# Seven half-block products for eight in a second feed-forward: one level of Strassen's scheme in a fused attention and feed-forward kernel

## The chip, the core and the metric

The kernel runs on one core of one Trainium2 chip. The metric is device time in microseconds (us) from start to end of one launch, as the median of three runs. A profile is one execution of its own, recorded by the hardware profiler; its times are read as us from the start of its span (first to last instruction). Engines are named as in the profile: PE is TensorE (matmuls), PEld its weight loads, DVE is VectorE, ACT is ScalarE, POOL is GpSimd, and SP issues the DMA transfers.

## What is computed

Three layers follow each other over 2304 tokens (4 sequences of 576).

```python
scores = q @ k.T / 8                       # 4 x 8 heads, 576 x 576, head size 64
scores = where(scores >= max - tau, scores, -1e9)
x = softmax(scores) @ v                    # heads joined: 2304 x 512
h = x @ w_in                               # 512 -> 1024
solu = h * softmax(h)
y = (layernorm(solu) * g_ln) @ w_out       # 1024 -> 512: y is 2304 x 512
h2 = y @ w2_in                             # 512 -> 2048
g = h2 * tanh(softplus(h2))                # "mish"
out = g @ w2_out                           # 2048 -> 512
```

The four weight matrices come as 64-bit floats. The kernel turns them into 32-bit floats on the chip.

## The kernel before

**An order made by a planner.** The code adds tasks (`plan.add`): an engine, a duration by a formula (`act`, `dve`, `gps`, `pe`, `dma`), the tasks it depends on, and the buffer slots that it takes or uses. `Plan.run` then tries `TURNS` rounds of list scheduling, forward and backward, with several weights (`WAITS`, `AVOID`), keeps the shortest order and writes the instructions in that order into the queue of each engine. So each engine's queue is a fixed order, and an instruction that waits holds all behind it. `ORDER` breaks ties between engines. Tasks marked `port=True` on VectorE and all GpSimd tasks are never planned at the same time.

**Words.** Each factor of the feed-forward matmuls is split into a high word (a copy that rounds to the type float32r, by ScalarE) and a low word (the difference, by VectorE or GpSimd). A product is then three matmuls: high by high, low by high, high by low.

**Attention** (`s_tile`, `turn`, `pv`) goes over 16 pairs of heads. **The first feed-forward** goes over 18 tiles of 128 tokens: `moe_h` (two output banks of 512 columns, 12 matmuls each), `layer_norm`, `moe_t` (transposes through PSUM into `LH`, `LL`) and, for each pair of tiles, `moe_y` (8 pieces of 12 matmuls, 256 wide), whose result `y` leaves as `yh` and `yl` to `y_hi`, `y_lo` in DRAM. Its pieces stand between those of attention where the order allows it.

**The second feed-forward** goes over four quarters `q` of the 2048 features, and within each over units of tokens `work`: for the first quarter six units of 256 tokens (`U0`), which may run while the first feed-forward isn't finished, then units of up to 512. `ff_in(c)` multiplies 48 matmuls into banks `h2` (`L981`), applies mish (`L986`), splits into `gh` (`L987`) and `gl` (`L988`); `ff_out(c)` multiplies 48 into `o2` (`L1007`), and VectorE adds the result into `acc` (`L1031`), which holds all output in SBUF, or ScalarE copies it there for the first quarter. The six early units put theirs by way of `part` in DRAM.

**The weights** of all four matrices are fetched in blocks of 128 by 256 by `convert` (`L474` to `L497`: two ScalarE or VectorE operations, three of VectorE, one addition by GpSimd). Those of the second feed-forward are converted in `split_w2(q)`, right into the tiles `AH`, `AL`, `BH`, `BL` of their quarter (`L924`, `L926`), of which two sets stand in turn.

**Buffers open in three steps**, as one stage's memory is given to the next: `open_a` when attention's scores are done (weight tiles of even quarters), `open_b` when its outputs are stored (buffers of the early units and six banks of PSUM), `open_c` when the first feed-forward has stored `y` (the rest).

## Time and profile before

| | |
|---|---|
| median of three runs | 913.32 us (912.12 to 914.53) |
| the profiled execution | 908.55 us |
| its span | 906.8 us |
| TensorE busy | 889.1 us |
| VectorE busy | 528.1 us |
| ScalarE busy | 522.0 us |
| GpSimd busy | 335.7 us |
| bytes moved by DMA | 122.28 MB, mean 135 GB/s |

Busy time counts an engine's instructions once where they overlap, so the sum of single durations is larger. A matmul's shown duration runs past the start of the next: what one costs is read from the distance of starts, or from a group in the chain of work that ended last (so many in so many us). The share of the DMA engines is a mean over sixteen.

### The profile page before, as it was taken

Reading aid. Unit: us, or ns where it says so; the run is one execution under the profiler, and the core shown is the slowest. Engines: PE = TensorE matmul, PEld = TensorE weight load, DVE = VectorE, ACT = ScalarE, POOL = GpSimd, SP = SyncE. Lnnn points to the kernel's source line nnn. Section 1 sums busy time; section 2 is a strip of 40 time slices with the busy share of each in tenths; the row PEclk is TensorE's granted clock in tenths of the full one; section 3 lists DMA queues with packets and bytes.
Section 4 is the critical chain, followed back from the end, with each engine's and each line's share of the span. In section 5 each row is a group of like instructions: output and inputs, shape, how many; then the busy total and the mean of one; then the engine's idle time right before and its main releaser. Section 6 shows DMA issues by size and latency. Waiting matters only on the chain.

```text
span 906.8 us, 15748 instructions
## 1 busy us (share of the span) xinstructions
PE 889.1 (98%) x5611; PEld 735.7 (81%) x5611; DVE 528.1 (58%) x1204; ACT 522.0 (58%) x1096; POOL 335.7 (37%) x470
## 2 busy tenths in 40 slices
PE   8889999999999999999999999999999999999998
PEld 4555566779878888979999999988888888888887
DVE  7998787888886787567743421445544354222222
ACT  5888788989887777567854533554432333221220
POOL 2565657787555553255411102343331234000000
PEclk9999999999999999999999999999999999999999
DMA  5434534355334431247333138954444444223211
GB/s 190 157 132 150 163 133 133 96 162 159 104 120 128 133 103 54 71 118 249 103 117 105 59 105 270 362 182 151 157 158 139 151 151 140 93 71 120 89 47 70
DMA packets 102173, 122.28 MB, mean 135 GB/s; under 512 B 11968, under 2 KB 75728, under 8 KB 102096
## 3 DMA queue, kind: packets, MB, share of 16 engines
q1 hardware_dynamic: 101952, 121.28, 41.7%
q8 instruction: 44, 0.72, 0.3%
q14 instruction: 33, 0.27, 0.1%
q10 hardware_dynamic: 144, 0.00, 0.0%
HBM read 99.16 MB, written 22.09 MB: 134 GB/s over the span
## 4 chain that ended last, share of the span: by engine, by line
PE 87%; ACT 3%; DVE 2%; POOL 1%; DMA 1%; issue 1%; SPq 0%; DVEq 0%; POOLq 0%; ACTq 0%
PE o L1007 16%; PE h L981 15%; PE p_mo L817 11%; PE p_mo L748 10%; PE p_ta L697 7%; PE h2b L981 7%; PE o2b L1007 6%; PE p_ta L649 5%; PE st L614 4%; PE st L605 3%; PE p_mo L796 2%; ACT e L621 1%; DVE e L624 1%; PE p_ta L652 1%; DVE m L620 1%
## 5 line engine op out<-in xcount | busy, mean ns | idle before, releaser
L497 POOL TENSOR_TENSOR cf<-cf,cl 128x256 uint32<-128x256 uint32 x96 | 74.4, 777 | 134.7 <-DVE cf L495 107.5
L624 DVE SCALAR_TENSOR_TENSOR e<-st,m,e 128x576 f32<-128x576 f32 x132 | 106.8, 815 | 26.7 <-ACT e L621 17.1
L620 DVE TENSOR_REDUCE m<-st 128x1 f32<-128x576 f32 x132 | 97.9, 752 | 24.8 <-PE st L614 13.7
L621 ACT ACTIVATE e<-st,m 128x576 f32<-128x576 f32 x132 | 97.2, 742 | 24.8 <-DVE m L620 23.2
L649 PE MATMUL p_ta<-ident,e 128*128 128x128 f32 x576 | 86.2, 277 | 5.4 <-ACT ey L632 2.4
L649 PEld LDWEIGHTS p_ta<-ident,e 128*128 128x128 f32 x576 | 65.7, 140 | 26.0 <-ACT ey L632 6.6
L817 PE MATMUL p_mo<-LH,W2H 128*128 128x256 f32 x288 | 83.4, 290 | 0.0
L817 PE MATMUL p_mo<-LL,W2H 128*128 128x256 f32 x288 | 81.5, 283 | 0.0
L817 PE MATMUL p_mo<-LH,W2L 128*128 128x256 f32 x288 | 81.4, 283 | 0.0
L623 POOL TENSOR_SCALAR m<-m,cs 128x1 f32<-128x1 f32 x144 | 42.4, 296 | 87.4 <-DVE m L620 75.5
L1031 DVE TENSOR_TENSOR acc<-acc,o 128x512 f32<-128x512 f32 x36 | 24.8, 688 | 70.5 <-PE o L1007 70.3
L748 PE MATMUL p_mo<-W1H,XH 128*128 128x512 f32 x144 | 60.8, 422 | 0.0
L986 ACT ACTIVATE n<-h 128x512 f32<-128x512 f32 x36 | 21.5, 597 | 63.6 <-PE h L981 62.5
L817 PEld LDWEIGHTS p_mo<-LH,W2H 128*128 128x128 f32 x288 | 55.1, 191 | 2.0 <-issue 1.9
L748 PE MATMUL p_mo<-W1H,XL 128*128 128x512 f32 x144 | 56.5, 393 | 0.0
L748 PE MATMUL p_mo<-W1L,XH 128*128 128x512 f32 x144 | 56.3, 391 | 0.0
L1007 PE MATMUL o<-gh,BH 128*128 128x256 f32 (+1 forms) x178 | 56.0, 315 | 0.0
L1007 PE MATMUL o<-gh,BL 128*128 128x256 f32 (+1 forms) x178 | 55.7, 313 | 0.0
L1007 PE MATMUL o<-gl,BH 128*128 128x256 f32 (+1 forms) x178 | 55.7, 313 | 0.0
L817 PEld LDWEIGHTS p_mo<-LH,W2L 128*128 128x128 f32 x288 | 55.2, 192 | 0.2
L817 PEld LDWEIGHTS p_mo<-LL,W2H 128*128 128x128 f32 x288 | 55.1, 191 | 0.0
L484 ACT ACTIVATE cl<-cr 128x256 uint32<-128x256 uint32 x96 | 40.9, 433 | 22.1 <-DMA cr<-w_in 16.4
(157 smaller groups left out, 2550.7 us busy)
## 6 DMA issues: line engine op xcount, KB each, us to landing
y5h<-y_hi SPq DMA_DIRECT2D x26, 512.0 KB, 4.8
y5l<-y_lo SPq DMA_DIRECT2D x26, 512.0 KB, 6.8
cr<-w_in SPq DMA_DIRECT2D x48, 256.0 KB, 3.6
cr<-w_out SPq DMA_DIRECT2D x48, 256.0 KB, 3.0
V<-v SPq DMA_DIRECT2D x16, 320.0 KB, 3.5
Q<-qq SPq DMA_DIRECT2D x16, 320.0 KB, 3.2
K<-kk SPq DMA_DIRECT2D x16, 320.0 KB, 2.9
y2h<-y_hi SPq DMA_DIRECT2D x10, 512.0 KB, 4.7
```

Source lines behind the costliest of these rows:

```text
L484: t2 = add("ACT", act(CW), lambda: SC.activation(cl.tile, cr.tile[:, :, 0], ACTF.Copy, scale=2.0 ** -29), [t_f], [cl], [cr])
L497: t = add("POOL", gps(CW), lambda: G.tensor_tensor(cf.tile, cf.tile, cl.tile, ALU.add), [t4, t2], use=[cl, cf])
L620: t = add("DVE", dve(S), lambda: V.tensor_reduce(m.tile[:, 2:3], x(), AX.XY, ALU.max, negate=True), [t], [m], [st])
L621: a = add("ACT", act(S, True) + 0.1, lambda: SC.activation(et(), x(), ACTF.Exp, bias=m.tile[:, 2:3]), [t], [e] if h == 0 else (), [st, m, ...
L623: b = add("POOL", 0.26, lambda: G.tensor_scalar(m.tile[:, 1:2], m.tile[:, 2:3], -1.0, nt8, ALU.mult, ALU.add), [t], use=[m])
L624: t = add("DVE", dve(S) + 0.06, lambda: V.scalar_tensor_tensor(et(), x(), m.tile[:, 1:2], et(), ALU.is_ge, ALU.mult, accum_out=sr.tile[:, ...
L649: TE.transpose(tp.tile[:, k * 128:(k + 1) * 128], e.tile[:, o:o + 128], ident)
L697: TE.matmul(acc.tile[h * 64:h * 64 + 64, :w], v.tile[:, k, h], r, start=(k == 0), stop=(k == KT))
L748: TE.matmul(h.tile, l.tile[:, kt], r[:, kt, j * 512:(j + 1) * 512], start=(kt == 0 and x == 0), stop=(kt == KD - 1 and x == 2))
L817: TE.matmul(y.tile[:, :PN], l[:, k, cs], r.tile[:, k], start=(k == 0 and x == 0), stop=(k == KF - 1 and x == 2))
L981: TE.matmul(h.tile[:, a * w:(a + 1) * w], l.tile[:, k, s], r.tile[:, k], start=(k == 0 and x == 0), stop=(k == KD - 1 and x == 2))
L1007: TE.matmul(o.tile[:, a * w:(a + 1) * w], l.tile[:, k, ds], r.tile[:, k % n * w:(k % n + 1) * w], start=(k == 0 and x == 0), stop=(k == FG ...
```

## The change

The second feed-forward's two products are made by one level of Strassen's scheme (in Winograd's form). A factor is cut in two by two half blocks. Seven products of sums of half blocks stand for the eight products of half blocks, and the four blocks of the result are sums of the seven; partial sums grow in the PSUM bank itself, where a bank is copied out and the next product is added to it.

- **Units.** Tokens go in 3 units of 768 (two halves of 384: each matmul is 384 wide). The 2048 features go in 8 groups of 256. `VISITS` gives the order of units and quarters: unit 0 with quarters 0 and 1, unit 1 with 1 and 0, unit 2 with all four, then units 0 and 1 again with 3 and 2, and 2 and 3.
- **Block sums of the weights** are made once, when they are converted: four VectorE operations on blocks of 128 by 128 give seven blocks from four, stored to `w2c` in DRAM as one word. They no longer wait for a tile of their quarter. A chunk that is loaded (`load_w`) is split there: the high word by ScalarE, the low one by VectorE (A) or GpSimd (B). The last group or quarter loaded is kept for the next visit.
- **Block differences of y** are made in `moe_y` by four VectorE operations for 256 tokens, split into two words (`words7`) and stored to `yc`; a visit loads seven chunks of its unit.
- **`ff_in`** makes seven products of six matmuls in three banks; ScalarE copies three partial sums, VectorE adds in three, mish is applied to four blocks, four differences give the seven blocks of the second factor (three by VectorE, one by GpSimd), and each is split in two words.
- **`ff_out`** makes 14 products of six matmuls in six banks. Every product's bank is added into `acc` (or copied, where it is the first); `acc` holds one unit, goes to `part` between the two visits of units 0 and 1, and to `out` at the end.
- **Buffers.** `open_a` now waits for the end of attention and gives the banks, the A and y chunks; `open_b` waits for the last matmuls of `moe_h` (`HT`) and gives the buffers for the banks' copies and the words of the second factor; `open_c` waits for the last `y` and gives B chunks, `acc` and two more banks.
- The planner runs 40 rounds for 80, with one more weight, and breaks ties with TensorE first. `convert` has four fetch buffers for two.

The core of the diff:

```diff
-    TURNS = 80
+    TURNS = 40
     WAITS = 20.0, 250.0
     ISSUE, LATENCY = 0.65, 0.92
-    LOAD, AVOID = 1.3, (3.0, 150.0)
+    LOAD, AVOID = 1.3, (3.0, 30.0, 150.0)
...
-    ORDER = {e: k for k, e in enumerate(("SP", "ACT", "POOL", "DVE", "PE", "-"))}
+    ORDER = {e: k for k, e in enumerate(("PE", "DVE", "ACT", "POOL", "SP", "-"))}
...
-    NG = 4
-    FG = KF2 // NG
     NP = NT // PN
     M0 = 4
-    LATE = 0
-    U0 = 6
+    TU = 3 * PN
+    TH = TU // 2
+    NU = NT // TU
+    RAW = (0,1)
+    NQ = KF2 // 2
...
+    yc = [dram.tile([7, 128, 2, TU // PN, 2, 128], F32, name=f"yc{u}") for u in range(NU)]
+    part = [dram.tile([KD, 128, TU], F32, name=f"part{u}") for u in range(NU)]
+    w2c = [[dram.tile([128, 7, 1 if x in RAW else 2, 256], F32, name=f"w2c{x}{g}") for g in range(NQ)] for x in range(2)]
...
-    b_cr = buf("cv", "cr", [128, CW, WN], U32 if WN == 2 else F32, 2)
+    b_cr = buf("cv", "cr", [128, CW, WN], U32 if WN == 2 else F32, 4)
...
+            if into:
+                at, n, slots, order = into
+                wide = lambda x: x.tile.rearrange("p (a b) -> p a b", a=n)
+                return add("POOL", gps(CW), lambda: G.tensor_tensor(at(), wide(cf), wide(cl), ALU.add), [t4, t2],
+                           slots if order is None else [], [cl, cf, *slots], order=[order])
...
+    def words7(eng, e, cost, hi, x, t, dst, n, split):
+
+        out = []
+        for c in split:
+            m = n * (c.stop - c.start)
+            a = add("ACT", act(m), lambda c=c: SC.activation(hi.tile[:, c], f(x.tile[:, c]), ACTF.Copy), [t], [] if out else [hi], [hi, x])
+            b = add(e, cost(m), lambda c=c: eng.tensor_tensor(x.tile[:, c], f(x.tile[:, c]), f(hi.tile[:, c]), ALU.subtract), [a], use=[hi, x], port=True)
+            out.append((a, b))
+        return [add("SP", dma(128 * 7 * n * 4), lambda w=w, y=y: D(dst(w), f(y.tile)), [o[w] for o in out], use=[y]) for w, y in ((0, hi), (1, x))]
+
+    WLO = V, "DVE", dve
+    ALL, HALVES = (slice(0, 7),), (slice(0, 4), slice(4, 7))
+    b_ws, b_wh = buf("ws", "ws", [128, 7, 128], F32R, 2), buf("ws", "wh", [128, 7, 128], F32R, 2)
+    for g in range(NQ):
+        for x, src in enumerate((w2_in, w2_out)):
+            WST[x, g] = []
+            for k in range(2):
+                ws, wh, ts = b_ws.new(), b_wh.new() if x not in RAW else None, []
+                for j in range(2):
+                    at = lambda ws=ws, j=j: ws.tile.bitcast(U32)[:, j:7:4 + j]
+                    row, cols = ((2 * j + k) * 128, (g * 256, g * 256 + 128)) if x == 0 else ((2 * g + j) * 128, (k * 128, 256 + k * 128))
+                    ts.append(convert(src, row, cols, None, into=(at, 2, [ws], ts[0] if ts else None)))
+                add7 = lambda o, a, b, op, ws=ws: (dve(128), lambda: V.tensor_tensor(*(f(ws.tile[:, z]) for z in (o, a, b)), op))
+                t = chain("DVE", [add7(3, 4, 6, ALU.add), add7(2, 3, 0, ALU.subtract), add7(5, 1, 2, ALU.subtract), add7(4, 0, 4, ALU.subtract)], ts, use=[ws], port=True)
+                if x in RAW:
+                    WST[x, g].append(add("SP", dma(128 * 7 * 512), lambda ws=ws, x=x, g=g, k=k: D(w2c[x][g][:, :, 0, k * 128:k * 128 + 128], f(ws.tile)), [t], use=[ws]))
+                    continue
+                WST[x, g] += words7(*WLO, wh, ws, t, lambda w, x=x, g=g, k=k: w2c[x][g][:, :, w, k * 128:k * 128 + 128], 128, ALL)
...
-        yh, yl = (b.new() for b in b_yy)
-        a = add("ACT", act(PN, True), lambda: SC.activation(yh.tile, y.tile[:, :PN], ACTF.Copy), [t], [yh], [y])
-        b = add("DVE", dve(PN), lambda: V.tensor_tensor(yl.tile, y.tile[:, :PN], f(yh.tile), ALU.subtract), [a], [yl], [yh, y])
-        YST.setdefault(p, []).append(add("SP", dma(PN * 512), lambda: D(y_hi[p][cs, :], f(yh.tile)), [a], use=[yh]))
-        YST[p].append(add("SP", dma(PN * 512), lambda: D(y_lo[p][cs, :], f(yl.tile)), [b], use=[yl]))
+        if c == 0:
+            YS[p] = b_ys.new(), []
+        ys, ts = YS[p]
+        j, k = divmod(c, 2)
+        ts.append(add("ACT", act(PN, True), lambda: SC.activation(
+            f(ys.tile)[:, j:j + 5:4, k * 128:k * 128 + 128], y.tile[:, :PN].rearrange("p (a b) -> p a b", a=2), ACTF.Copy),
+            [t], [] if c else [ys], [y, ys], order=ts[:1]))
+        if c < KD - 1:
+            return
+        sub = lambda o, a, b: (dve(256), lambda: V.tensor_tensor(*(f(ys.tile[:, z]) for z in (o, a, b)), ALU.subtract))
+        t = chain("DVE", [sub(3, 4, 0), sub(2, 5, 3), sub(4, 5, 4), sub(6, 1, 2)], ts, use=[ys], port=True)
+        u, z = divmod(p, TU // PN)
+        dst = lambda w: yc[u].rearrange("c q w z k n -> q c w z (k n)")[:, :, w, z]
+        YST[p] = words7(V, "DVE", dve, b_yh.new(), ys, t, dst, 256, HALVES)
...
+    NA, NB, NL, NR, NX, NC, NF = 9, 22, 14, 15, 3, 6, 9
+    o_a = opens(open_a, end_c3 + list(XST.values())[-2:] + [t for x in b_any.slots for t in x.users if t.eng != "PE"])
+    o_b = opens(open_b, [o_a] + HT[-4:])
+    o_c = opens(open_c, [o_b] + [t for ts in YST.values() for t in ts][-4:] + [t for ts in TEV.values() for t in ts][-16:])
+    ff = [Bank(lambda n=n: P[n], f"{n}{k}") for n, m in (("hoa", 6), ("hob", 2)) for k in range(m)]
+    for k in ff:
+        k.after = o_a if k in ff[:6] else o_c
+    b_f = Buf(None, "", [128, 512], F32, banks=ff)
+    b_a, b_b = (buf(p, n, [128, 2, 256], F32R, k) for p, n, k in (("fa", "A7", NA), ("fc", "B7", NB)))
+    b_y, b_yx = (buf(p, n, [128, 2, TU // PN, 2, 128], F32R, k) for p, n, k in (("fa", "y7", 7), ("fc", "y7x", NX)))
+    ring_y = [b_y] * 7
+    b_gl, b_gh = buf("fb", "gl", [128, TH], F32R, NL), buf("fb", "gh", [128, TH], F32R, NR)
+    b_gf = buf("fb", "gf", [128, TH], F32, NF)
+    b_ac = buf("fc", "acc", [128, TU], F32, NC)
...
+    words = (0, 0), (1, 0), (0, 1)
+    YC, GC, AC, CO, PA, AL, BL = ({} for _ in range(7))
+    VISITS = (0, (0,1)), (1, (1,0)), (2, (0,1,2,3)), (0, (3,2)), (1, (2,3))
...
+    def load_w(b, x, g, c, gate):
+        w = b.new()
+        if x in RAW:
+            t = add("SP", dma(128 * 1024), lambda: D(f(w.tile[:, 1]), w2c[x][g][:, c, 0]), WST[x, g] + [gate], [w])
+            t = add("ACT", act(256), lambda: SC.activation(w.tile[:, 0], f(w.tile[:, 1]), ACTF.Copy), [t], use=[w])
+            eng, n, cost = SPLIT[x]
+            return w, add(n, cost(256), lambda: eng.tensor_tensor(w.tile[:, 1], f(w.tile[:, 1]), f(w.tile[:, 0]), ALU.subtract), [t], use=[w], port=True)
...
+    def ff_in(z, g):
+        A = AL.pop(g, None) or [load_w(b_a, 0, g, c, o_a) for c in range(7)]
+        AL.clear()
+        AL[g] = A
+        X, Y, Z = (b_f.new() for _ in range(3))
...
+        p1 = p(0, X, True, [])
+        c1 = copy(X, s[0], p1)
+        p2 = p(1, Y, True, [])
+        g11 = mish(s[0], plus(Y, s[0], [c1, p2]))
+        p6 = p(2, X, False, [c1])
+        c2 = copy(X, s[1], p6)
+        p5 = p(3, Z, True, [])
+        p7 = p(4, X, False, [c2])
+        c3 = copy(X, s[2], p7)
+        c22 = plus(Z, s[2], [c3, p5])
+        p3 = p(5, Z, False, [c22])
+        g12 = mish(s[1], plus(Z, s[1], [c2, p3]))
+        g22 = mish(s[2], c22)
+        p4 = p(6, X, False, [c3])
+        g21 = mish(s[5], p4, X)
+        t1 = minus(0, s[3], s[1], s[0], [g11, g12], True)
+        t3 = minus(1, s[1], s[2], s[1], [t1, g22])
+        t2 = minus(2, s[4], s[2], s[3], [t1, g22], True)
+        t4 = minus(3, s[6], s[5], s[4], [t2, g21], True)
+        out = {}
+        for c, x, first, deps in ((0, 0, g11, [t1]), (5, 2, g22, [t2, t3]), (3, 3, t1, [t2]), (4, 1, t3, []),
+                                  (2, 4, t2, [t4]), (1, 5, g21, [t4]), (6, 6, t4, [])):
+            h, l, x = b_gh.new(), b_gl.new(), s[x]
+            a = add("ACT", act(TH), lambda h=h, x=x: SC.activation(h.tile, full(x), ACTF.Copy), [first], [h], [h, x])
+            e, cost, eng = ("POOL", gps, G) if c in LOWP else ("DVE", dve, V)
+            out[c] = h, l, add(e, cost(TH), lambda h=h, l=l, x=x, eng=eng: eng.tensor_tensor(l.tile, full(x), f(h.tile), ALU.subtract), [a, *deps], [l], [h, l, x], port=True)
+        GC[z, g] = out
...
+        def put(e, i, t, x, deps, first):
+            ac = AC[v, e, i]
+            to = lambda: ac.tile.rearrange("q (z t n) -> q z t n", t=2, n=128)[:, :, t]
+            fr = lambda: x.tile[:, :TH].rearrange("q (z n) -> q z n", n=128)
+            if begins and first and not more[0]:
...
+        E = range(2)
+        p1 = [p(0, e, X[e], True, []) for e in E]
+        r1 = [put(e, 0, 0, X[e], [p1[e]], True) for e in E]
+        p2 = [p(1, e, Y[e], True, []) for e in E]
+        [put(e, 0, 0, Y[e], [p2[e], r1[e]], False) for e in E]
+        p6 = [p(2, e, X[e], False, [r1[e]]) for e in E]
+        r2 = [put(e, 0, 1, X[e], [p6[e]], True) for e in E]
+        p5 = [p(3, e, Z[e], True, []) for e in E]
+        p7 = [p(4, e, X[e], False, [r2[e]]) for e in E]
+        r3 = [put(e, 1, 1, X[e], [p7[e]], True) for e in E]
+        a2 = [put(e, 1, 1, Z[e], [p5[e], r3[e]], False) for e in E]
+        p3 = [p(5, e, Z[e], False, [a2[e]]) for e in E]
+        [put(e, 0, 1, Z[e], [p3[e], r2[e]], False) for e in E]
+        p4 = [p(6, e, X[e], False, [r3[e]]) for e in E]
+        [put(e, 1, 0, X[e], [p4[e]], True) for e in E]
+        if ends:
+            for i in range(2):
+                for e in E:
+                    r0 = (e + 2 * i) * 128
+                    to = (lambda e=e, i=i: part[u][e + 2 * i]) if more[1] else (lambda r0=r0: out[r0:r0 + 128, u * TU:(u + 1) * TU])
+                    PA[u, e, i] = add("SP", dma(512 * TU), lambda e=e, i=i, to=to: D(to(), AC[v, e, i].tile),
...
+    MINUS = [{'D': ('DVE', dve(TH)), 'P': ('POOL', gps(TH))}[k] for k in 'DPDD']
+    SPLIT = ((V, "DVE", dve),(G, "POOL", gps))
+    LOWP = ()
+    for z, (_, qs) in enumerate(VISITS):
+        load_y(z)
+        for q in qs:
+            for g in (2 * q + 1, 2 * q) if q == qs[0] and z else (2 * q, 2 * q + 1):
+                ff_in(z, g)
+            ff_out(z, q)
```

## Rows read from the trace of the kernel before

**Rows 1.** The page, first part: busy us, share, instructions.

```profile
PE 889.1 (98%) x5611; PEld 735.7 (81%) x5611; DVE 528.1 (58%) x1204; ACT 522.0 (58%) x1096; POOL 335.7 (37%) x470
```

**Rows 2.** The longest wait of TensorE: us, times, longest us.

```profile
PE st L605 <- DVE e L624: 4.1, 4, 2.0
```

**Rows 3.** Busy time by stage, granted clock, DMA share, GB/s.

```profile
0.00:125.00 125.00, 112.30 (x728) 66.26 (x729) 105.85 (x252) 98.77 (x223) 65.58 (x125) 1.00 0.50 160
125.00:400.00 275.00, 273.94 (x1956) 223.44 (x1956) 210.73 (x476) 223.80 (x479) 157.65 (x212) 1.00 0.36 113
400.00:550.00 150.00, 150.00 (x1107) 142.49 (x1104) 76.29 (x181) 85.30 (x167) 41.51 (x42) 1.00 0.39 124
550.00:907.00 357.00, 352.82 (x1827) 303.46 (x1826) 135.19 (x296) 114.10 (x230) 70.91 (x94) 1.00 0.45 148
```

**Rows 4.** The chain that ended last: start, us, what.

```profile
534.50 11.52 PE p_mo L817 x96
...
655.85 2.72 PE o2b L1007 x12
```

**Rows 5.** TensorE groups by form (second feed-forward): count, busy us, mean ns.

```profile
L981 PE MATMUL h<-y5h,AH 128*128 128x512 f32 x124 | 48.3, 390 | 0.0
...
L981 PE MATMUL h<-y2h,AH 128*128 128x256 f32 x136 | 39.1, 287 | 0.0
```

**Rows 6.** The timeline of VectorE from 400 us: start, us, instruction.

```profile
402.17 0.69 DVE L802 TENSOR_TENSOR LL<-p_mo,LH 128x512 fp32r<-128x512 f32 x1 [1.09 <-ACT LH L801]
402.78 0.15 DVE L766 RECIPROCAL ln<-ln 128x1 f32<-128x1 f32 x1
...
411.44 0.42 DVE L828 TENSOR_TENSOR yl<-p_mo,yh 128x256 fp32r<-128x256 f32 x1
411.78 0.41 DVE L495 SCALAR_TENSOR_TENSOR cf<-cr,cz 128x256 uint32<-128x256 uint32 x1
```

**Rows 7.** VectorE's groups by form: busy us, mean ns, idle before.

```profile
L495 DVE SCALAR_TENSOR_TENSOR cf<-cr,cz 128x256 uint32<-128x256 uint32 x96 | 46.4, 490 | 8.4 <-POOL AL L926 5.5
...
L1031 DVE TENSOR_TENSOR acc<-acc,o 128x512 f32<-128x512 f32 x36 | 24.8, 688 | 70.5 <-PE o L1007 70.3
...
L988 DVE TENSOR_TENSOR gl<-n,gh 128x512 fp32r<-128x512 f32 x28 | 19.8, 717 | 23.6 <-ACT gh L987 23.6
```

**Rows 8.** The timeline of ScalarE, two stretches at 500 and 549 us.

```profile
502.44 1.09 ACT L801 ACTIVATE LH<-p_mo 128x512 fp32r<-128x512 f32 x2 [0.23 <-PE p_mo L796]
...
549.43 0.71 ACT L924 ACTIVATE AH<-cf 128x256 fp32r<-128x256 f32 x2
```

**Rows 9.** ScalarE's groups by form.

```profile
L801 ACT ACTIVATE LH<-p_mo 128x512 fp32r<-128x512 f32 x36 | 21.3, 599 | 9.3 <-PE p_mo L796 8.6
...
L924 ACT ACTIVATE AH<-cf 128x256 fp32r<-128x256 f32 x32 | 12.6, 410 | 8.7 <-POOL cf L497 8.7
```

**Rows 10.** GpSimd's groups by form.

```profile
L926 POOL TENSOR_TENSOR BL<-cf,BH 128x256 fp32r<-128x256 f32 x32 | 24.9, 788 | 19.6 <-ACT BH L924 19.6
...
L737 POOL TENSOR_TENSOR XL<-XR,XH 128x512 fp32r<-128x512 f32 x18 | 23.2, 1291 | 50.0 <-ACT XH L736 50.0
```

**Rows 11.** Busy time in stretches of 25 us, two of them.

```profile
50.00:75.00 25.00, 22.25 (x151) 13.03 (x149) 24.31 (x58) 21.59 (x52) 14.68 (x26) 1.00 0.45 143
...
575.00:600.00 25.00, 25.00 (x151) 22.38 (x150) 10.46 (x31) 11.65 (x25) 9.64 (x13) 1.00 0.83 280
```

**Rows 12.** The timeline of SP's queue from 549 to 556 us.

```profile
551.81 0.50 SPq L968 DMA_DIRECT2D y5l<-y_lo  x1
```

**Rows 13.** DMA issues: count, KB each, us to landing.

```profile
y_hi<-yh SPq DMA_DIRECT2D x36, 128.0 KB, 1.9
...
out<-acc SPq DMA_DIRECT2D x18, 256.0 KB, 2.1
```

**Rows 14.** The timelines of VectorE and GpSimd at 35 us.

```profile
35.68 1.48 DVE L495 SCALAR_TENSOR_TENSOR cf<-cr,cz 128x256 uint32<-128x256 uint32 x1
...
35.47 1.41 POOL L711 TENSOR_TENSOR xo<-xo,rx 128x576 f32<-128x576 f32 x1 [0.68 <-DMA rx<-rd]
```

More of the change, by code (lines that the diff above doesn't have):

```diff
@@ L507, in halves @@
         return put
[L509 to L512 removed]
+    W1T, W2T, WST = {}, {}, {}
     for c in range(0, FF, CW):
@@ new lines, with product, go @@
+    b_ac = buf("fc", "acc", [128, TU], F32, NC)
+    def product(e, terms, x, new, deps, use, stop, order=None):
+        def go():
+            steps = [(l, r) for a, b in terms for l, r in zip(a(), b())]
+            for n, (l, r) in enumerate(steps):
+                TE.matmul(x.tile[:, :TH], l, r, start=new and n == 0, stop=stop and n == len(steps) - 1, skip_group_check=True)
+        return add("PE", pe(3 * len(terms) * e, TH), go, deps, [x] if new else [], [x, *use], order=[order])
+    words = (0, 0), (1, 0), (0, 1)
```

267 lines of the change are left out of this document (89 added, 178 removed).

## The prediction

> **What bounds the kernel now.** I read the page's first part, then the waits of TensorE, then the stage windows, then the chain. TensorE is busy 889.1 of 906.8 us, no other engine over 58% [rows 1]. The reader is to see in the waits that TensorE hardly ever waits for data: the longest total is 4.1 us, in attention [rows 2]. The stage windows say where the 17.7 us of gaps lie: 12.7 in the first 125 us, 1.1 up to 400, none between 400 and 550, and 4.2 in the last window, which is the end [rows 3]. In the chain the second feed-forward is one dense run of matmul groups at two prices: twelve 512-wide ones in 2.72 us (226.7 ns each) and 96 of 256 columns in 11.52 us (120.0 ns each) [rows 4]. The price is linear: 256 more columns cost 106.7 ns, and 13.3 ns come with each matmul. The granted clock is 1.00 in every window [rows 3], the upper level (2.4 GHz), so nothing is to be had there. What shortens the kernel is work taken off TensorE, as long as the other engines keep its queue fed.
>
> **The matmuls.** By the code's list of units there are 13 of 512 tokens and 10 of 256, each with 48 matmuls in and 48 out for its quarter; [rows 5] show one form of each width (124 and 136 of them, a part). That is 1248 x 0.2267 + 960 x 0.120 = 398.1 us. After: 24 pairs of unit and 256-wide feature group make 7 products of 6 matmuls going in (1008), and 12 visits to a quarter make 14 products of 6 coming out (1008): 2016, all 384 wide. No row has that width. Per column as the 512-wide ones it would be 170.0 ns (342.7 us, a gain of 55.4); as the 256-wide ones 180.0 (362.9, a gain of 35.2). On the line between them it is 173.4 ns, 349.5 us: **a gain of 48.6 us**. I take the line, since both widths fit it exactly. It sits on the path: 906.8 - 48.6 = 858.2.
>
> **VectorE.** Each operation's length overlaps the next: a 512-wide subtraction of 0.69 us is followed after 0.61, a 256-wide one of 0.42 after 0.34 [rows 6]. So 384 costs 0.475, 128 about 0.205. Removed: 72 subtractions for gl, 54 additions into acc (both 512) and 36 for yl (256) [rows 6, 7]: 44 + 33 + 12 = 89 us. Added: 24 x 13 of 384 in ff_in (3 additions from PSUM, 3 differences, 7 low words) = 148; 144 additions into acc = 68; 140 splits of A chunks at 256 (20 loads of a group by 7) = 48; 128 block sums of weights at 128 = 26; block differences of y, 36 at 256 = 12, and their low words, 9 x (1024 + 768) = 18. Together 320. VectorE goes from 528 to 759 us, 88% of 858. It lies beside TensorE's work; that is the cover, and a thin one.
>
> **ScalarE and GpSimd.** Two LH copies of 512 take 1.09 us and two AH copies of 256 take 0.71, single ones 0.60 and 0.41: steps of 0.49 and 0.30, so 0.40 for 384 [rows 8, 9]. Removed 144 + 18 of 512 and 64 of 256 (99 us); added 24 x 14 of 384 (134), 252 splits (76), 24 copies into acc (10), y's high words (19): 522 to 662 us, 77%. GpSimd loses 64 subtractions of 256 at 0.79 (50 us), gains 112 for B (88) and 24 of 384 (between 0.79 and 1.29, about 1.04; 25) [rows 10]: 336 to 399 us, 46%. Both are hidden by TensorE; without that cover they would cost their time, but VectorE would be first to show it.
>
> **DMA and SP's queue.** The 64 fetches of second weights move ahead, past attention's loads, with 32 stores of 459 KB behind them; y's stores grow from 9.4 to 16.5 MB. The share there is 0.36 to 0.50 [rows 3], so I cost them at nothing. In the second feed-forward the loads are 18.4 (A) + 14.7 (B) + 27.5 (y) + 3.1, the stores 3.1 + 4.7: 71.6 MB in some 350 us, 205 GB/s. The window from 575 to 600 us moved 280 GB/s at a share of 0.83 with TensorE busy 25.00 of 25 [rows 11]: nothing. SP issues some 315 transfers there; one in a row of others took 0.50 us [rows 12], so 158 us of 350.
>
> **New waits.** (1) Attention and the first feed-forward share VectorE with block sums and conversions that were mostly made later. Below: nothing, since VectorE was busy 24.31 of 25 us once [rows 11] while filling such holes. Above: 17 us, as 759 at the 0.85 of the first window [rows 3] would be 893 in all, half of its 35 us above 858 put to this stage. I take 4: after 125 us attention hides such things well. (2) The first six units of the second feed-forward (576 matmuls of 0.12, 69 us) may now run between pieces of the first; afterwards they can't, as their buffers open with the last of its input matmuls. Below nothing, since 11.52 us of output products stand between one tile's normalization and the next; above 18 us, were each of 18 transposed banks (two for each of the last nine tiles) to wait out a copy of 0.6 us and the start of its subtraction. I take 2. (3) At the turnover the output product of unit 0 waits for the last y: copy, four differences, two splits, store, B load and split, by the steps above and landings of 1.9 us [rows 13] some 12 us. Ready meanwhile are two or three groups of ff_in at 7.3 us. Between 0 and 12; I take 3. (4) Inside a product chain an accumulator must be copied before the next product adds to it: four hand-offs for each ff_in, eight for each ff_out, 192 in all, at two sources of products that can fill in for each other. Behind the waiting matmul stand all later ones, of both, in one queue. Nothing below; the slower rival prices the top. I take 3. (5) The last store is 384 KB instead of 256, which took 2.1 us [rows 13]: 1 us at the end.
>
> Sum: 858.2 + 4 + 2 + 3 + 3 + 1 = 871.2 us of span. Around the span lie 908.55 - 906.8 = 1.75 us, so 873.0 for the profiled execution; the median of the runs, 913.32, is 4.8 above it, so **878 us**.
>
> **A rule against the change.** A VectorE operation of 0.41 us took 1.48 where it started 0.21 us into a GpSimd one of 1.41, and ended 0.28 after it [rows 14]. The Trainium skill ("SBUF — State Buffer", Who interferes with whom) says that a VectorE instruction with two SBUF inputs and a GpSimd instruction that reads SBUF lock each other out for the whole instruction; by that rule the trace agrees. As a mechanism of this kernel, from rows alone: L495 averages 490 ns [rows 7] where 410 is its length with nothing beside it (the last of [rows 6]), so 80 ns are lost for each. The operations with both inputs in SBUF are 240 in ff_in, 140 splits and 36 + 128 sums and differences: 544 x 0.08 = 44 us on VectorE, 803 in all. That is the first rival.
>
> **Rivals.** First, VectorE becomes the bound. For it: 803 of 858 us is a share of 0.94, and TensorE already waits where VectorE holds 0.85 [rows 3]. Against it: 0.97 was reached for 25 us [rows 11], and the fullest demand can be moved in time, since weights needed only by the third unit may be summed late. At 0.90 the span is 892 and the median 899; the range 0.89 to 0.92 gives 879 to 909. Second, slower: the hand-offs of (4). A product of 6 takes 1.04 us; the copy takes 0.49, plus what is queued on ScalarE (77% full) and the signal both ways. If TensorE stands at each of the 192, the gain less the other new waits, 48.6 - 10, is spent from 0.20 us each; at 0.25 us each, 48 us, the span is 858.2 + 10 + 48 = 916, the median 923. For it speaks that the banks are eight and ff_out alone takes six; against it that between a product and the next on its bank stand one (going in) or three others (coming out), and that the waits of today show none of this kind [rows 2]. Third, the change doesn't do what it says: 384-wide matmuls, read with a stride, at the price of 512-wide ones: 2016 x 0.2267 = 457 us, 59 more than now: 906.8 + 59 + 6.5 = 972. Against it: both present widths lie on one line [rows 4].
>
> **How the numbers follow.** A measurement of this kernel tells 0.3%, 2.7 us, from no change. TensorE stays the bound with small gaps: 0.58, with its own range of 860 (every wait at nothing, 170.0 ns each: 906.8 - 55.4 + 1 + 6.5 = 859) to 890. VectorE the bound, 890 to 910: 0.22. Hand-offs, slower: 0.12. Wide matmuls: 0.02. Between, within 0.3%: 0.04; below 860: 0.02. Faster 0.58 + 0.22 + 0.02 = 0.82, same 0.04, slower 0.14. From 860 to 912 lies 0.82.
>
> **What would show it.** Matmul groups of six in 1.04 us and 2016 of them; TensorE idle some 30 us, of which 12 to 17 are still in the first 125; VectorE's busy time near 750 to 800; no wait on DMA in the second feed-forward over a few us. The prediction is wrong if a chain through ScalarE or VectorE stands between products, if VectorE's share before the turnover passes 0.92 with gaps on TensorE beside it, or if a six takes more than 1.1 us.

## The result and the profile after

The changed kernel takes 901.12 us (median of 4 runs, 899.40 to 902.93) against 912.72 for the kernel before in the same measurement: a ratio of 0.9876, with a 95% interval of 0.9839 to 0.9914. It is faster, by 1.2% where 3.9% were forecast, and stands some 2 us from what the first rival gave (899). The profiled execution took 899.40 us, its span is 897.5, the granted clock 0.997.

The page of the changed kernel, its first part and the head of the chain, beside [rows 1]:

```profile
PE 850.5 (95%) x5419; PEld 737.8 (82%) x5419; DVE 804.8 (90%) x1820; ACT 644.9 (72%) x1492; POOL 433.2 (48%) x542
...
PE 48%; DVE 24%; ACT 7%; DMA 5%; issue 4%; POOL 2%; SPq 0%; DVEq 0%; ACTq 0%; POOLq 0%
```

TensorE has 192 matmuls fewer, VectorE stands at 90%, and a quarter of the chain that ended last is VectorE's, where it was 2% before. The chain shows the new matmuls at their price (start, us, what), and two windows behind 750 us show them dense, beside [rows 4, 11]:

```profile
565.53 3.12 PE hoa L946 x18
568.65 1.04 PE hob L946 x6
```

```profile
775.00:800.00 25.00, 25.00 (x146) 25.00 (x146) 24.34 (x51) 15.11 (x38) 6.66 (x8) 1.00 0.51 161
800.00:825.00 25.00, 25.00 (x146) 24.94 (x146) 20.59 (x41) 13.84 (x35) 4.01 (x6) 1.00 0.69 234
```

18 in 3.12 us are 173.3 ns each; 2016 of them make 349.4 us, 48.7 less than the 398.1 of before. The span fell by only 9.3. So 39 us went into waits, where the prediction had 13. The stage windows say where to look, the kernel before first, then the changed one:

```profile
375.00:750.00 375.00, 375.00 (x2357) 337.70 (x2356) 181.21 (x434) 182.43 (x374) 110.88 (x132) 1.00 0.49 159
```

```profile
375.00:500.00 125.00, 120.47 (x795) 104.87 (x794) 113.72 (x310) 82.85 (x178) 49.33 (x51) 1.00 0.75 242
500.00:625.00 125.00, 112.51 (x659) 106.02 (x658) 113.25 (x233) 87.21 (x219) 50.99 (x58) 0.99 0.74 243
625.00:750.00 125.00, 118.41 (x662) 113.92 (x661) 121.50 (x263) 84.64 (x223) 54.99 (x58) 1.00 0.61 192
```

Before, TensorE was busy in all of these 375 us. Now it is idle for 23.6 of them, while VectorE is busy for 348.5, where it had 181.2 before. A matmul that starts late behind one whose modelled end is late too leaves no idle time, so I also went through TensorE's timeline matmul by matmul: the time from each start to the next, less the undisturbed step of the same form in that trace, added up by stage. It is my own working, good to a few us, and the experiments below are compared by it; not every run is in it:

```
us lost between starts    0-375  375-500  500-625  625-750  750-end   span
before                    143.9      6.9      0.8      0.2      0.3  906.8
changed                   137.2     18.0     19.9     10.8      2.3  897.5
A's low words cut         140.6     18.3     14.3      4.9      1.7  889.3
B's low words cut         139.1     18.3     11.2      4.6      1.3  884.2
gl cut                    141.2     18.1     14.0      5.9      0.5  889.5
A, B and gl cut           136.9     18.0      8.6      2.9      0.3  876.3
half of the block sums    147.3     16.9      9.3      2.2      2.2  885.8
B split on VectorE        145.1     20.6     11.1      2.6      3.2  887.6
before, no early units    135.7     21.6     16.1      0.3      0.2  927.7
changed, old search       140.9     20.9     21.5     18.0     11.6  918.4
```

Against the kernel before, the change lost 11 us more from 375 to 500 us, 30 more in the two stages behind, and 2 more at the end. The first feed-forward's last matmul starts at 527.6, so the 30 lie mostly in the second. In the first 375 us this working gives 6.7 less, while TensorE stood idle there for 18.7 us instead of 13.8; so nothing is made of that stage. The VectorE groups by form and GpSimd's costliest show what became of single operations, beside [rows 7, 10]:

```profile
L1031 DVE TENSOR_TENSOR gl<-gf,gh 128x384 fp32r<-128x384 f32 x168 | 97.2, 613 | 1.8 <-ACT gh L1029 1.6
L972 DVE TENSOR_TENSOR A<-A 128x256 fp32r<-128x256 f32 x140 | 68.6, 508 | 2.9 <-ACT A L970 2.9
L1067 DVE TENSOR_TENSOR acc<-acc,hoa 128x384 f32<-128x384 f32 x108 | 58.4, 547 | 15.8 <-PE hoa L946 11.2 <-ACT acc L1065 3.9
L1003 DVE TENSOR_TENSOR gf<-gf 128x384 f32<-128x384 f32 x72 | 54.0, 751 | 1.6 <-ACT gf L999 1.3
L555 DVE TENSOR_TENSOR ws<-ws 128x128 f32<-128x128 f32 x128 | 52.9, 418 | 0.0
```

```profile
L972 POOL TENSOR_TENSOR B<-B 128x256 fp32r<-128x256 f32 x112 | 92.7, 852 | 76.2 <-ACT B L970 60.1 <-DMA B<-w2c 8.5 <-issue 4.8
```

Three of these are 384 wide: the addition that reads a bank of PSUM (L1067) averages 547 ns, the differences with both inputs in SBUF 613 (L1031) and 751 (L1003). One stretch shows why, in the timelines of VectorE, GpSimd, TensorE and ScalarE:

```profile
548.63 0.82 DVE L555 TENSOR_TENSOR ws<-ws 128x128 f32<-128x128 f32 x1
549.37 0.82 DVE L500 TENSOR_SCALAR cz<-cz 128x256 uint32<-128x256 uint32 x1
550.11 0.82 DVE L555 TENSOR_TENSOR ws<-ws 128x128 f32<-128x128 f32 x1
550.86 0.94 DVE L502 SCALAR_TENSOR_TENSOR cf<-cr,cz 128x256 uint32<-128x256 uint32 x1
...
556.57 0.54 DVE L996 TENSOR_TENSOR gf<-gf,hoa 128x384 f32<-128x384 f32 x1
```

```profile
545.81 7.33 POOL L972 TENSOR_TENSOR B<-B 128x256 fp32r<-128x256 f32 x9 [0.45 <-ACT B L970]
553.10 1.19 POOL L1003 TENSOR_TENSOR gf<-gf 128x384 f32<-128x384 f32 x1
554.26 3.73 POOL L972 TENSOR_TENSOR B<-B 128x256 fp32r<-128x256 f32 x5
```

```profile
557.16 1.80 PE L946 MATMUL hoa<-y,A 128*128 128x384 f32 x6 [2.14 <-DVE gf L996]
```

```profile
557.14 0.53 ACT L999 ACTIVATE gf<-gf 128x384 f32<-128x384 f32 x1 [4.96 <-DVE gf L996]
```

GpSimd converts B chunks without a pause. VectorE, which has conversions and block sums of weights in its queue, gets one operation in between two of GpSimd's: a block sum takes 0.82 us where the same line took 0.28 at 544.02, with GpSimd idle. Behind these operations in VectorE's queue stands the addition from PSUM (L996) that frees a bank. It runs at 556.57; ScalarE had stood 4.96 us for it and TensorE 2.14. Before, the longest total of TensorE's waits was one in attention [rows 2].

### The profile page after: what moved, and what is told of

The parts are those of the page before. It is cut to its first block, busy times and chain, and to the rows that moved or that the text cites. A ratio compares the mean times of both kernels' runs of the same rounds, so it can differ in the third digit from the quotient of the medians.

```text
span 897.5 us, 16969 instructions
## 1 busy us (share of the span) xinstructions
PE 850.5 (95%) x5419; PEld 737.8 (82%) x5419; DVE 804.8 (90%) x1820; ACT 644.9 (72%) x1492; POOL 433.2 (48%) x542
## 4 chain that ended last, share of the span: by engine, by line
PE 48%; DVE 24%; ACT 7%; DMA 5%; issue 4%; POOL 2%; SPq 0%; DVEq 0%; ACTq 0%; POOLq 0%
PE hoa L946 16%; PE p_mo L853 6%; PE hob L946 6%; PE p_mo L783 6%; PE p_ta L732 5%; DMA A<-w2c 3%; PE p_ta L684 3%; PE st L649 3%; DVE gl L1031 3%; DVE ws L555 2%; PE st L640 2%; DVE acc L1067 2%; DVE gf L1003 2%; DVE A L972 2%; DVE e L659 2%
## 5 line engine op out<-in xcount | busy, mean ns | idle before, releaser
L946 PE MATMUL hoa<-gh,B 128*128 128x384 f32 x512 | 131.9, 337 | 6.0 <-DVE acc L1067 3.9
L972 POOL TENSOR_TENSOR B<-B 128x256 fp32r<-128x256 f32 x112 | 92.7, 852 | 76.2 <-ACT B L970 60.1
L946 PE MATMUL hoa<-y,A 128*128 128x384 f32 x534 | 107.2, 340 | 9.2 <-ACT gf L993 5.0
L655 DVE TENSOR_REDUCE m<-st 128x1 f32<-128x576 f32 x132 | 97.2, 750 | 18.7 <-PE st L649 9.1
L946 PEld LDWEIGHTS hoa<-y,A 128*128 128x128 f32 x534 | 92.8, 188 | 13.5 <-ACT gf L993 8.4
L946 PEld LDWEIGHTS hoa<-gh,B 128*128 128x128 f32 x512 | 91.9, 188 | 10.1 <-DVE acc L1067 6.0
L1031 DVE TENSOR_TENSOR gl<-gf,gh 128x384 fp32r<-128x384 f32 x168 | 97.2, 613 | 1.8 <-ACT gh L1029 1.6
L1003 POOL TENSOR_TENSOR gf<-gf 128x384 f32<-128x384 f32 x24 | 30.8, 1282 | 116.1 <-DVE gf L1003 106.1
L946 PE MATMUL hoa<-gl,B 128*128 128x384 f32 x256 | 85.9, 336 | 0.2 <-DVE gl L1031 0.2
L1029 ACT ACTIVATE gh<-gf 128x384 fp32r<-128x384 f32 x168 | 77.7, 513 | 3.1 <-POOL gf L1003 2.1
L1067 DVE TENSOR_TENSOR acc<-acc,hoa 128x384 f32<-128x384 f32 x108 | 58.4, 547 | 15.8 <-PE hoa L946 11.2
L972 DVE TENSOR_TENSOR A<-A 128x256 fp32r<-128x256 f32 x140 | 68.6, 508 | 2.9 <-ACT A L970 2.9
```

Of the source, the lines that this page charges most:

```text
L655: t = add("DVE", dve(S), lambda: V.tensor_reduce(m.tile[:, 2:3], x(), AX.XY, ALU.max, negate=True), [t], [m], [st])
L946: TE.matmul(x.tile[:, :TH], l, r, start=new and n == 0, stop=stop and n == len(steps) - 1, skip_group_check=True)
L972: return w, add(n, cost(256), lambda: eng.tensor_tensor(w.tile[:, 1], f(w.tile[:, 1]), f(w.tile[:, 0]), ALU.subtract), [t], use=[w], port= ...
L1029: a = add("ACT", act(TH), lambda h=h, x=x: SC.activation(h.tile, full(x), ACTF.Copy), [first], [h], [h, x])
L1031: out[c] = h, l, add(e, cost(TH), lambda h=h, l=l, x=x, eng=eng: eng.tensor_tensor(l.tile, full(x), f(h.tile), ALU.subtract), [a, *deps], ...
L1067: d = add("DVE", dve(TH), lambda: V.tensor_tensor(to(), to(), fr(), ALU.add), deps + [CO.get((v, e, i, t))], use=[ac, x])
```

## The experiments

I set up three theories against each other. One: VectorE, by its own work and by what it waits behind GpSimd, sets the pace from 375 to 750 us (the first rival). Two: the hand-offs between ScalarE, VectorE and TensorE do, whatever the load (the second rival). Three: chunks and y arrive late. Each run was timed beside the kernel before, whose own median lay between 907.48 and 912.72 us from one measurement to the next; so runs of different measurements are compared by their ratios to it. The changed kernel's ratio is 0.9876.

**One low word at a time, in the same order of work.** The subtraction is made for 8 columns only, for A in the first run and for B (`x == 1`) in the second; the plan still costs the whole of it, so nothing else moves.

```diff
-            return w, add(n, cost(256), lambda: eng.tensor_tensor(w.tile[:, 1], f(w.tile[:, 1]), f(w.tile[:, 0]), ALU.subtract), [t], use=[w], port=True)
+            m = 8 if x == 0 else 256
+            return w, add(n, cost(256), lambda: eng.tensor_tensor(w.tile[:, 1, :m], f(w.tile[:, 1, :m]), f(w.tile[:, 0, :m]), ALU.subtract), [t], use=[w], port=True)
```

> The same order of instructions; the low word of each A chunk is made for 8 of its 256 columns, the rest keeps the raw sum (140 VectorE operations of 0.51 us become short, some 55 us, all of them in the second feed-forward). Theory 1, VectorE is the bound there (its own work and its waits behind GpSimd): TensorE's gaps between 500 and 750 us, 19 us, mostly close, and the span falls by 10 to 20 us from 898. Theory 2, TensorE waits for the hand-off of each PSUM bank to a ScalarE copy, whatever VectorE does: under 4 us. Theory 3, chunks come late by DMA: no change.

> The same order; the low word of each B chunk is made for 8 of 256 columns (112 GpSimd operations of 0.85 us become short, some 70 us of GpSimd, none of VectorE). Theory 1 with the lock: VectorE's operations with two SBUF inputs fall towards their free lengths (A's split 0.51 to 0.44, the differences in gf 0.75 to 0.60), its busy time falls by 15 to 30 us, the span by 8 to 15. Theory 1 without a lock (VectorE's own work alone) and theories 2 and 3: within 3 us.

Cutting A's (VectorE's) gave 889.81 us, 0.9799 (0.9776 to 0.9821); cutting B's (GpSimd's) 886.53, 0.9766 (0.9744 to 0.9788). B's gain lies where I expected it, A's below (8 us of span for 10 to 20). GpSimd's work counts at least as much as VectorE's own: with it gone VectorE's A split fell from 508 to 424 ns and the differences from 751 to 645, with no instruction of VectorE touched. Theories two and three expected under 4 us from either run, so neither is the main part.

**The third word product left out**: a third of the second feed-forward's matmuls, 672 of 173.3 ns, 116 us of TensorE's work.

```diff
+            steps = steps[:4] if e == 2 else steps[:2] + steps[3:5]
```

> The same order; the third of the three word products (high by low) is left out of the second feed-forward: 672 of 2016 matmuls less, 116 us of TensorE's work. If TensorE is the bound with small gaps, the span falls by 90 us or more. Theory 1: VectorE was busy 341 of 375 us from 500 to 875, so the span can fall by little more than its own holes and waits, 20 to 40 us, and VectorE stands above 0.95 there. Theory 2: a chain of seven products and four copies loses a third of its product time, 50 to 80 us.

882.88 us, 0.9721 (0.9699 to 0.9742): of 116 us TensorE gave back 16 in the span (881.3), where theory one had expected 20 to 40. The window of the three stages together:

```profile
375.00:750.00 375.00, 310.33 (x1732) 274.08 (x1731) 349.51 (x807) 254.40 (x622) 156.99 (x170) 0.94 0.70 227
```

TensorE has 65 us to spare and VectorE is as busy as before (349.51 against 348.48; a share of 0.93, not above 0.95 as expected). In these stages TensorE is not the bound. The granted clock fell to 0.94 here, so part of what TensorE had left to do took longer, which this run does not separate.

**The low word of the second factor**, left out with a new plan (the diff), and cut to 8 columns in the old order, with the high word's tile read in its place:

```diff
-            out[c] = h, l, add(e, cost(TH), lambda h=h, l=l, x=x, eng=eng: eng.tensor_tensor(l.tile, full(x), f(h.tile), ALU.subtract), [a, *deps], [l], [h, l, x], port=True)
+            out[c] = h, h, a
```

> The low word of the second factor isn't made; the high word is read in its place, so TensorE's matmuls are as many (168 VectorE operations less, 97 us; the order is planned anew). Theory 1: the second feed-forward runs on TensorE alone, its gaps of 24 us from 500 us on shrink to some 5, and the span falls by 15 to 25 us. Theory 2: the hand-offs stand as before, under 6 us. Theory 3: none.

> The same order as the changed kernel; the low word of the second factor is made for 8 of 384 columns and the high word is read in its place (168 VectorE operations of 0.61 us become short, some 85 us, of which about 50 before 750 us; TensorE's work the same). Theory 1 (from 375 to 750 us VectorE is the bound, 348 of 375 us): the 24 us of gaps there close by 12 to 20 us. Rival (the planner's order and the late loads set the stage, VectorE only follows): under 5 us, as with the run that left these operations out and planned anew (its median fell by about 4).

893.52 us, 0.983 (0.9801 to 0.9859), and 889.32, 0.9785 (0.9765 to 0.9804). Both came out smaller than I had expected of theory one (15 to 25 us and 12 to 20). The first has a new plan, with the DMA share from 500 to 625 us at 0.90; whether that is the reason was not tried. The second, in the same order, agrees with the cut of A's words.

**Half of the block sums**: features of the second half use those of the first; the plan is new.

```diff
+            if g >= NQ // 2:
+                WST[x, g], w2c[x][g] = WST[x, g - NQ // 2], w2c[x][g - NQ // 2]
+                continue
```

> The second half of the features takes the block sums of the first half, so 32 of 64 conversions and 64 of 128 block sums are left out; everything behind them is as it was (planned anew). Theory 1, with the load named: between 375 and 750 us some 118 us of VectorE's 348 are conversions and block sums of these weights. Half of them gone frees some 55 us, and the span falls by 15 to 25. If the gaps there came from loads or hand-offs of the products themselves: under 5.

887.27 us, 0.9763 (0.9744 to 0.9782). I had expected 15 to 25 us; the span fell by 12. The sums and their conversions cost what a low word costs. DMA's work fell with them (a share of 0.57 from 500 to 750 us for 0.68).

**All three cuts together**, in the order of the changed kernel.

> The same order as the changed kernel; the low words of A, of B and of the second factor are all made for 8 columns (the three same-order cuts together; the high word is read for the second factor's low one). Theory 1: the cuts ease the same bound, so they don't add up: alone they gave 7, 10 and 8 us, together they give 15 to 22, as no more than some 25 us of gaps lie between 500 and 750 us; the loss from 375 to 500 stays near 18 us. If each had a gap of its own: 25 us or more.

880.55 us, 0.9704 (0.9678 to 0.973), span 876.3. The three stages:

```profile
375.00:750.00 375.00, 364.01 (x2224) 344.00 (x2223) 275.28 (x833) 266.95 (x647) 106.09 (x172) 1.00 0.74 243
```

VectorE is down to 73%, and two losses remain: 18.0 us from 375 to 500, and 11.5 in the two stages behind. So theory one, the work of VectorE and GpSimd together, explains some 19 of the 30 us there. On the 18 these cuts say little, since hardly any of the operations that they shorten run in that stage (11 of A's 140 splits and none of B's): VectorE is still busy for 110.82 of its 125 us, after 113.72. With half of the block sums VectorE is at 103.17 there and the loss is 1.1 less. In the first run without the second factor's low word, which the table leaves out, the new plan has VectorE at 99.81 us there, and the same working gives 4 to 5 us less.

**What the 18 may be: the kernel before without its early units.** These are the six units of the second feed-forward that could run between pieces of the first. In the kernel before 348 matmuls of the second feed-forward start ahead of the last one of the first, in the changed kernel 78, in this run none.

```diff
-    U0 = 6
+    U0 = 0
```

> The kernel before with no early units (U0 = 0): nothing of its second feed-forward can stand between the pieces of the first any more, all else as it was; 6 units of 256 tokens become 3 of 512, which by itself saves 576 x 120.0 - 288 x 226.7 ns = 3.8 us. Theory 1b: the 11 us that TensorE loses more from 375 to 500 us in the changed kernel, and which no run on VectorE's load in the second feed-forward has moved (16.9 to 18.3 us in each), come from that missing filler: the time rises by 5 to 15 us, with gaps on TensorE between 400 us and the turnover. Rival (they come from VectorE's conversions and block sums there): no rise, a fall of 4 us.

930.26 us, 1.0238 (1.0219 to 1.0257). Its windows:

```profile
375.00:500.00 125.00, 117.72 (x785) 101.29 (x784) 71.41 (x189) 70.49 (x159) 51.39 (x53) 1.00 0.28 87
500.00:625.00 125.00, 112.23 (x561) 94.84 (x560) 41.57 (x96) 46.91 (x95) 24.15 (x33) 0.96 0.53 169
```

The rise is larger than the 5 to 15 us that I expected. With VectorE at 57% the old kernel loses 21.6 us from 375 to 500, as much as the changed one, and 16.1 behind, 10.2 of it in one wait at the turnover for y to come back from DRAM. So missing filler alone is enough for a loss of this size, with VectorE far from full. That it makes up all of it in the changed kernel is not shown: no run gives that kernel its filler back, and the run with VectorE at 99.81 us in this stage lost less.

**Less conversion for more DMA.** One operand's weights are stored as two words and their low words made once, with a few buffers fewer to make room: A's on VectorE, A's on GpSimd (the second edit of the diff is this run's alone), and in the third run B's on VectorE (`RAW = (0,)`).

```diff
-    RAW = (0,1)
+    RAW = (1,)
-    WLO = V, "DVE", dve
+    WLO = G, "POOL", gps
```

> The whole computation. A's chunks are stored as two words, split once when they are summed (16 pairs of splits of 896 columns for 140 of 256 on VectorE), so a load brings 256 KB for 128; one fetch buffer, one copy buffer and one word buffer are given up for the room. VectorE loses some 50 us net, of them 20 or so before 750 us; DMA gains 25 MB. Theory 1: 4 to 10 us faster than the changed kernel. Theory 3 (loads are late): slower.

> As the run before, with the low words of A made by GpSimd (16 operations of some 2 us). VectorE's own work falls by 70 us. If VectorE's own work is what counts: faster than the run before by some 5 us. If its time locked behind GpSimd counts as much: no faster, since each of the long GpSimd operations holds VectorE up.

> The whole computation; B's chunks are stored as two words, split once by VectorE when they are summed, and GpSimd makes no low words at load (93 us less); one fetch buffer's worth of room is given up elsewhere (one word buffer, one copy buffer). VectorE gets 16 pairs of splits, 32 us, before 750 us, and loses waits behind GpSimd; DMA gains 25 MB. Theory 1 with the lock: 0 to 8 us faster than the changed kernel. Theory 3: slower.

899.81 us, 0.9883 (0.9853 to 0.9914); 911.87, 1.0029 (1.0012 to 1.0047); 899.87, 0.9895 (0.9868 to 0.9923). In the first the DMA share rises from 0.68 to 0.88 from 500 to 750 us and VectorE is busy for 224.03 us there instead of 234.75; it is as fast as the changed kernel. That misses both what theory one expected (4 to 10 us faster) and what theory three did (slower), and since less of VectorE and more of DMA came together, it decides between neither. The second moves the low words from VectorE to GpSimd and loses 12 us against the first, as theory one says. The third is a miss too: B's 112 conversions are gone from GpSimd, and nothing was won. By the same working the new plan lost 7.0 us less from 500 to 750 and 9.5 more in the first 375; why it placed its work so was not tried apart.

Late loads stay a rival for a part. From 500 to 625 us loads of A are 18.6% of the changed kernel's chain, its largest share there, the longest two (start, us, what) being

```profile
582.16 6.28 DMA A<-w2c
609.58 7.10 DMA A<-w2c
```

TensorE works on other products beside these two, and with all three cuts such loads are still 14.3% of the chain there. What they cost no run shows.

**B's low words on VectorE**, the whole computation; a second run has the last of the four differences there too (`'DDDD'` for `'DPDD'`).

```diff
-    SPLIT = ((V, "DVE", dve),(G, "POOL", gps))
+    SPLIT = ((V, "DVE", dve),(V, "DVE", dve))
```

> The whole computation; the low words of B are made by VectorE for GpSimd (planned anew). VectorE gets 112 x 0.34 = 38 us more work of its own, and GpSimd loses 93 us, so that waits behind it, some 70 us of VectorE's length in the second feed-forward and the block sums, become fewer by half. Theory 1 with the lock: within 6 us of the changed kernel, either way. If VectorE's own work alone counted: 15 us or more slower.

> As the run with B's low words on VectorE, and the fourth difference of ff_in too (24 operations of 1.2 us on GpSimd become 24 of 0.475 on VectorE, 11 us more of VectorE's work). GpSimd then has nothing in the second feed-forward but the late conversions. If waits behind GpSimd are worth more than VectorE's own work: 0 to 4 us faster than that run. If VectorE, 246 of 250 us busy there from 500 to 750 us, has no room left: 3 to 8 us slower.

889.25 us, 0.9783 (0.9763 to 0.9803), faster than both kernels, by more than the 6 us against the changed one that I had allowed, and 891.06, 0.9816 (0.979 to 0.9842), neither faster nor the 3 to 8 us slower that I had expected of a full VectorE. Its groups by form, and its window of the two stages, where the changed kernel had TensorE at 230.91, VectorE at 234.75:

```profile
L1031 DVE TENSOR_TENSOR gl<-gf,gh 128x384 fp32r<-128x384 f32 x168 | 88.7, 557 | 0.5 <-ACT gh L1029 0.2
...
L972 DVE TENSOR_TENSOR A<-A 128x256 fp32r<-128x256 f32 x140 | 57.4, 426 | 0.7 <-ACT A L970 0.7
...
L972 DVE TENSOR_TENSOR B<-B 128x256 fp32r<-128x256 f32 x112 | 43.8, 411 | 2.3 <-ACT B L970 2.3
```

```profile
500.00:750.00 250.00, 243.85 (x1435) 236.33 (x1434) 246.08 (x616) 181.12 (x460) 53.29 (x42) 1.00 0.73 239
```

VectorE takes 112 operations more, 43.8 us, and is busy for 811.3 us instead of 804.8: 37 us of what it had been busy with was waiting. A split of 411 ns here cost 852 on GpSimd.

**The search.** The change also altered how the plan is searched (turns, margins, order of engines). Three runs take that apart: the changed kernel with the old search, the kernel before with the new one, and B on VectorE with the old one.

```diff
-    TURNS = 40
+    TURNS = 80
-    LOAD, AVOID = 1.3, (3.0, 30.0, 150.0)
+    LOAD, AVOID = 1.3, (3.0, 150.0)
-    ORDER = {... ("PE", "DVE", "ACT", "POOL", "SP", "-"))}
+    ORDER = {... ("SP", "ACT", "POOL", "DVE", "PE", "-"))}
```

> The changed kernel with the planner's old search: 80 rounds, two weights for three, ties as before. Nothing else. If the gaps come from the load on VectorE and its waits behind GpSimd, another search finds another order of the same work and the time stays within 5 us of the changed kernel. If the order that was found is the cause, it differs by 8 us or more.

> The kernel before with the three lines of the planner's search as the change has them (40 turns, three sets of due-time margins, the new order of engines). If the new search finds better orders for any kernel, this one should be faster than before by up to 1%, and part of the changed kernel's 1.24% is the search's, not Strassen's. If before's order was already near what its engines allow (TensorE busy 125.00 of 125 in most windows behind 375 us, 1.6 us of idle time there in all), it comes out within 0.5% of before, and the 3% between the changed kernel and its version with the old search is a matter of a plan with little slack on VectorE.

> Two edits together: the second operand's low words on VectorE, and the old search. If the loss with the old search is VectorE's (own work and waits behind GpSimd), taking GpSimd's conversions away gives back 10 to 14 us against the old search alone, as it did with the new one: ratio about 1.000 to 1.006. If the loss is the order itself, with PSUM readers queued late on ScalarE and VectorE, this stays at 1.010 to 1.020.

922.6 us, 1.0155 (1.0092 to 1.0218); 909.66, 1.0012 (0.9995 to 1.0029); 901.89, 0.992 (0.9891 to 0.9949). The search does nothing for the old scheme and decides for the new one between slower and faster. Theory one had expected 5 us of it at most; 8 or more was to mean that the order which was found is a cause of its own. Taking GpSimd's conversions away with the old search gives back 21 us, more than the 10 to 14 expected of theory one. One stall of that run, in the timelines of GpSimd, VectorE, ScalarE and TensorE:

```profile
741.58 7.20 POOL L972 TENSOR_TENSOR B<-B 128x256 fp32r<-128x256 f32 x1 [2.76 <-ACT B L970]
748.74 0.99 POOL L1003 TENSOR_TENSOR gf<-gf 128x384 f32<-128x384 f32 x1
```

```profile
741.55 0.42 DVE L972 TENSOR_TENSOR A<-A 128x256 fp32r<-128x256 f32 x1
741.88 0.55 DVE L1003 TENSOR_TENSOR gf<-gf 128x384 f32<-128x384 f32 x1
...
747.78 0.42 DVE L972 TENSOR_TENSOR A<-A 128x256 fp32r<-128x256 f32 x1
```

```profile
749.76 0.94 ACT L1029 ACTIVATE gh<-gf 128x384 fp32r<-128x384 f32 x2 [6.39 <-POOL gf L1003]
750.61 0.47 ACT L993 ACTIVATE gf<-hoa 128x384 f32<-128x384 f32 x1
```

```profile
751.13 2.29 PE L946 MATMUL hoa<-y,A 128*128 128x384 f32 x6 [7.07 <-ACT gf L993]
```

Here it is GpSimd that is kept out: one conversion of 0.79 us [rows 10] takes 7.20 while VectorE runs 16 operations with both inputs in SBUF, one behind the other. GpSimd's difference is late by that, ScalarE stands 6.39 us for it, and the copy that frees TensorE's bank stands behind that in ScalarE's queue. VectorE is not full in that run (314.78 of the 375 us). So part of the loss, there at least, is a queue in the wrong order and not a lack of time.

## Why the prediction was right in direction and wrong in size

- **The matmuls: right.** 173.3 ns measured, 173.4 forecast; a gain of 48.7 us, forecast 48.6. The third rival is out.
- **VectorE: the step that failed.** The sum took its 759 us as hidden under TensorE and left the waits behind GpSimd to a rival with a chance of 0.22. VectorE was busy 804.8 us (the rival: 803) at a share of 0.90 (the rival: 0.90), and the median, 901, lies in that rival's range. By the cuts this costs some 19 us. The argument against that rival, that 0.97 had been reached for 25 us, is where it went wrong: those 25 us stood alone in the first stage, TensorE was busy for only 22.25 of them in that same row [rows 11], and the demand here lasts. A share over the whole span hid it too. The block sums did not spread out: 100 of 128 ran between 375 and 750 us, and the share over these stages was 0.93. The sign that I named, over 0.92 before the turnover, looked too early: it was 0.91 from 375 to 500 us and 0.97 from 625 to 750.
- **The rule against the change: right.** The rule in the Trainium skill's "SBUF — State Buffer", Who interferes with whom, on VectorE operations with two SBUF inputs was set beside a rival's mechanism, and this trace agrees with it: 508 ns on average where the shortest took 410, 751 where it took 545, but 547 for an addition from PSUM. The 80 ns for each operation were near for the splits (98 measured) and the second factor's low words (68), and low for the differences (206).
- **Wait (2), the lost filler: mis-sized.** Forecast 2 us; TensorE lost 11 more from 375 to 500 us, and 15 more in the kernel before when its early units are taken away. How much of the 11 is filler and how much VectorE's load in that stage stays open. The upper bound I gave, 18, was nearer than my choice. Nor is the filler gone altogether: 36 matmuls of the second feed-forward start ahead of 500 us, 228 before.
- **Waits (3) and (4), turnover and hand-offs: too small, of the right kind.** 6 forecast; 10.5 left from 500 to 750 us over the kernel before when all three cuts are made, 4.9 of it in waits for ScalarE's copy of a bank (`L993`); the rest is not assigned. The second rival's 48 are out for the order that was found; with the old search the result did end on its side of zero (1.0155), by fewer and longer stalls than it had.
- **Wait (1), attention: open, and not what failed.** Forecast 4; the first 375 us lost 6.7 less than before by my working, and 4.9 more by TensorE's idle time.
- **DMA at nothing: not settled.** The share rose from 0.39 and 0.45 [rows 3] to 0.70, and loads of A lie on the chain; no run shows their cost. ScalarE 645 (662 forecast). GpSimd 433, 34 over the forecast, since it is kept out as well.
- **Not considered at all: the search.** I took the order of work as given. The search is worth 2.8% to this scheme and nothing to the old one.

With the forecast's terms replaced by these, 858.2 - 7 + 11 + 10.5 + 19 + 2 = 894, against a span of 897.5. These terms are read from the table of that very span, so the sum proves none of them. Where VectorE is out of the way the forecast's own sum nearly holds: 876.3 measured with all three cuts, 871.2 forecast. That is in part luck, as its wait (2) was too small and its wait (1), by the same table, too large. What stays open is how much of the 19 us is lack of time on VectorE and how much the order in its queue; the runs that plan anew move both at once.

## What to carry to other kernels

Count an engine's load by stage, and with the waits that its neighbour on a shared port adds, before calling it hidden: a change that moves work from a full TensorE to VectorE and GpSimd together can pay twice for it, as here. Try the operation on VectorE alone even when VectorE looks full; its busy time held 37 us of waiting. And when a restructuring takes away work that filled another stage's holes, price the filler from a run without it.

## What was unexpected of the hardware

- An operation with one tensor input was held up as well: the integer TENSOR_SCALAR at 549.37 took 0.82 us between GpSimd's conversions, where the same line's shortest took 0.28.
- The two patterns differ: in one the engines took turns (VectorE 0.81 to 1.10 us each time), in the other GpSimd waited 7.20 us through 16 operations of VectorE's. In the changed kernel the longest of GpSimd's 384-wide differences took 4.89 us, the shortest about 1.0.
- In the window of 25 us up to 750 us of the run with the old search the granted clock was 0.74, a mean between the two levels, with TensorE busy 11.25 us, and the first six matmuls behind its 7.07 us stall took 2.29 us, where the six behind the wait at 551.63 in the changed kernel took 1.31.
